# Row-sum reciprocals of an attention and feed-forward kernel: one VectorE reciprocal in place of a logarithm and an exponential on ScalarE

## The chip, the cores and the metric

The kernel runs on one core of a Trainium2 chip. The metric is the device time of one execution in microseconds. A core has a matrix engine (TensorE, PE in the profile, with its weight loads as PEld), VectorE (DVE), ScalarE (ACT), GpSimd (POOL) and a queue engine (SP). Each takes its own instructions strictly in order; they wait for one another by semaphores.

## The reference

The inputs are q, k, v of shape 8 x 8 x 576 x 64 (batch, head, row, depth), 16 further "beacon" keys and values for each head, and two weight matrices. The result is causal attention over beacons and rows, followed by a feed-forward layer with ELU:

```
scores = q @ concat(beacon_k, k).T / 8, causally masked (beacons are always seen)
a      = exp(scores - max);  a /= a.sum(-1) + 1e-9
x      = (a @ concat(beacon_v, v))  arranged as 4608 tokens x 512
out    = elu(x @ w_in) @ w_out      # w_in 512 x 2048, w_out 2048 x 512
```

The step that the change touches is the division by a.sum(-1), the row sums.

## The kernel before

The work runs through batches b = 0 to 7 and tiles t = 0 to 9 of the 4608 tokens. Attention of batch b fills x for the tiles that hold its tokens; the feed-forward steps of the tiles are interleaved with the attention of later batches. Nothing is left to a scheduler: a long string (lines 783 to 917) names each step in order, and each engine executes its own instructions in that order. The names below are those of the string.

Attention of a batch: `S` computes scores on PE (line 320) into PSUM tiles `sc`, `x` takes their exponentials on ACT (335) into `et`, `m` applies the causal mask on DVE (340). From batch 3 on, `D` adds up pieces of `et` on DVE (393) so that the row sums take fewer matmuls. `L` (line 401) computes the row sums on PE, as matmuls with a matrix of ones (377, 419), into the PSUM tile `lt`; each column of sums stands repeated over 32 partitions, so that it can be multiplied elementwise with the unnormalized output. `W` (448) computes that output on PE into `ut` (or `ub`, `ua`). `n` (429) is the step in question: it makes the reciprocals of the row sums in the SBUF tile `rl`. `M` (478, lines 471, 481, 488) multiplies `ut` by `rl` on DVE and writes `xT`, the input of the feed-forward part.

There are two groups of four heads per batch, so 16 steps `n`: one of 512 columns (`n.0.A`), one of 640 (`n.0.B`) and 14 of 576, all over 128 partitions in fp32.

Feed-forward: `F` (511) multiplies x by w_in on PE into PSUM banks `hps`; `e` (521) and `u` (526) take exponential and positive part on ACT; `k` (536) joins them on DVE into `gt`. For some tiles `r` (543) and `g` (548) do the second half on DVE instead. `G` (557), or for later tiles `Z` (578, sums on DVE), `Q` (621, matmuls) and `J` (630, 635, 637, copies and sums of results), multiply by w_out; the result goes out through the SP queue. The last two tiles use `P` (691), `K` (701, 704), `E`, `U`, `V` (713, 720, 730) in place of F, e, u, k.

What ties the engines: `e` and `r` tiles have three buffers, `hps`, `ops` and the scores' tag "S" two each. `lt` and `ut` are tiles of tag "S" and are read by DVE in `M`; `rl` has two buffers.

Of the kernel before, what the change touches and what calls it, by code (L numbers as in the profile page):

```python
# [11 lines left out]
AFT = mybir.ActivationFunctionType  # L12
# [5 lines left out]
def kernel(  # L18
# [11 lines left out]
    nc = tc.nc  # L30
# [110 lines left out]
    def load_v(b, js):  # L141
        if b not in vt:
            vt[b] = stage.tile([P, NKC, H, D], FP16, tag="v16", name="v16")
            nc.gpsimd.dma_start(  # L144
                out=vt[b][0:NB, 0, :, :], in_=beacon_v[b].rearrange("h n d -> n h d"))
        for j in js:
            r0 = NB if j == 0 else 0
            n = kc[j] - r0
            nc.gpsimd.dma_start(  # L149
                out=vt[b][r0:r0 + n, j, :, :],  # L150
                in_=v[b, :, ilo[j]:ilo[j] + n, :].rearrange("h s d -> s h d"),
            )
# [16 lines left out]
    for b in range(B):  # L169
        (nc.sync if b % 2 == 0 else nc.scalar).dma_start(  # L170
            out=bk32[NB * b:NB * (b + 1), :, :],
            in_=beacon_k[b].rearrange("h n d -> n h d"))
# [28 lines left out]
    @step  # L201
    def warm(n, rows=P):

        for _ in range(n):
            nc.tensor.matmul(
                out=w0, lhsT=zero[0:rows, 0:P], rhs=zero[0:rows, :], start=True, stop=True, skip_group_check=True)
# [221 lines left out]
    @step  # L428
    def n(b, g):
        src = lt[b, g]  # L430
        w = src.free_size()
        rl = rls[b, g] = attn.tile([P, 640], FP32, tag="rl", name="rl")
        dst = rl[:, 0:w]
        nc.scalar.activation(
            out=dst.rearrange("p (g c) -> p g c", g=2) if len(src.shape) == 3 else dst,
            in_=src, func=AFT.Ln, bias=0.0, scale=1.0)
        nc.scalar.activation(out=dst, in_=dst, func=AFT.Exp, bias=0.0, scale=-1.0)  # L437

    xt = {}

# [492 lines left out]
```

## Time and profile before

| | |
|---|---|
| median of 2 runs | 337.89 us (337.21 to 338.57) |
| span of the profiled execution (first to last instruction) | 335.3 us |
| busy: PE, ACT, DVE, POOL | 324.6, 282.5, 280.0, 87.9 us |
| granted TensorE clock, mean | 0.995 |

The profile gives the profiled execution by its span alone; its own time outside that is not shown. The span is 2.6 us below the median. Busy time is the time in which an engine executes; PE's is partly modelled, since matmuls overlap each other. "Idle before" is the idle time of an engine just ahead of an instruction, with the instruction of another engine that ended it.

### The profile page before, as it was taken

What the parts mean: (1) busy time and instruction counts of PE and PEld (TensorE: products, weight loads), DVE (VectorE), ACT (ScalarE), POOL (GpSimd) and SP (SyncE); (2) the same over time, 40 slices, a digit from 0 to 9 for tenths busy, and PEclk for the clock granted to TensorE, in tenths of its full rate; (3) what the DMA queues carried; (4) which work ended last, traced back from release to release, by engine and by line L of the source; (5) the groups of instructions that cost most, each with busy time, mean ns of one, the idle gap of its engine ahead of it and who ended that gap; (6) DMA issues with size and microseconds to landing.
All of it is one profiled execution on the core that took longest, in us unless ns stands there. A gap on an engine that the chain in (4) does not pass through costs nothing.

```text
span 335.3 us, 8722 instructions
## 1 busy us (share of the span) xinstructions
PE 324.6 (97%) x3561; PEld 206.8 (62%) x3561; DVE 280.0 (84%) x592; ACT 282.5 (84%) x460; POOL 87.9 (26%) x121
## 2 busy tenths in 40 slices
PE   7979899999999999999999999999999999999995
PEld 3546666454446555657555656556555888688784
DVE  3652988666899999997999889988999998998962
ACT  2998798899999999989898889897987677988930
POOL 8875749360049106500160060000000000000000
PEclk9997999999999999999999999999999999999999
DMA  9999999999939997996099495000101021010212
GB/s 114 146 174 178 165 186 186 157 147 176 149 52 170 175 139 61 171 149 105 33 140 139 104 100 139 3 33 31 39 27 34 31 65 65 31 65 31 65 63 96
DMA packets 129080, 34.65 MB, mean 103 GB/s; under 512 B 112912, under 2 KB 127504, under 8 KB 129040
## 3 DMA queue, kind: packets, MB, share of 16 engines
q0 software_dynamic: 94912, 18.49, 68.6%
q1 hardware_dynamic: 33408, 15.34, 21.2%
q8 instruction: 28, 0.46, 0.6%
q10 hardware_dynamic: 720, 0.26, 0.3%
q14 instruction: 12, 0.10, 0.1%
HBM read 37.22 MB, written 15.34 MB: 157 GB/s over the span
## 4 chain that ended last, share of the span: by engine, by line
PE 53%; DVE 20%; ACT 11%; DMA 7%; POOL 4%; issue 3%; ACTq 0%; POOLq 0%
PE ops L621 20%; PE hps L511 16%; DVE gt L536 6%; PE hps L691 6%; DVE qk L393 5%; ACT et L335 4%; ACT e L521 3%; PE sc L320 3%; PE ops L557 3%; ACT r L526 3%; PE ut L377 3%; DMA v<-in_v_dram 2%; DMA kst<-in_k_dram 2%; DMA w_out<-in_moe_w_out_dram 2%; DVE et L340 2%
## 5 line engine op out<-in xcount | busy, mean ns | idle before, releaser
L511 PE MATMUL hps<-xT,w_in 128*128 128x512 f16 (+1 forms) x544 | 120.2, 357 | 0.7 <-DMA w_in<-in_moe_w_in_dram 0.5
L335 ACT ACTIVATE et<-sc 128x1024 f16<-128x1024 f32 (+2 forms) x114 | 104.7, 978 | 5.3 <-PE sc L320 5.3
L621 PEld LDWEIGHTS <-gt 128*128 128x128 f16 x768 | 74.1, 98 | 18.7 <-issue 1.7
L521 ACT ACTIVATE e<-hps 128x512 f32<-128x512 f32 x120 | 72.5, 622 | 7.7 <-PE hps L511 5.9
L511 PEld LDWEIGHTS <-w_in 128*128 128x128 f16 x544 | 49.8, 98 | 45.3 <-issue 7.9
L536 DVE SCALAR_TENSOR_TENSOR gt<-e,r 128x512 f16<-128x512 f32 x108 | 71.9, 682 | 6.7 <-ACT r L526 4.4
L526 ACT ACTIVATE r<-hps 128x512 f16<-128x512 f32 x108 | 65.3, 623 | 7.7 <-PE hps L511 4.4
L621 PE MATMUL ops<-wt,gt 128*128 128x256 f16 x384 | 50.1, 273 | 0.0
L621 PE MATMUL ops<-w_out,gt 128*128 128x256 f16 x384 | 49.6, 273 | 0.4 <-DVE osb L635 0.3
L149 POOL DMA_DIRECT2D v<-in_v_dram x40 | 36.0, 1048 | 5.5 <-DMA w_out<-in_moe_w_out_dram 2.4
L340 DVE TENSOR_TENSOR et<-et,triu 128x512 f16<-128x512 f16 (+4 forms) x108 | 31.6, 331 | 1.5 <-ACT et L335 1.5
L578 DVE TENSOR_TENSOR gt<-gt 128x1024 f16<-128x1024 f16 x48 | 32.4, 684 | 0.3
L393 DVE TENSOR_TENSOR qk<-qk,et 128x672 f16<-128x672 f16 (+2 forms) x60 | 21.8, 368 | 0.9
L377 PEld LDWEIGHTS <-v 128*32 128x32 f16 (+1 forms) x800 | 17.0, 96 | 8.7 <-issue 0.8
L377 PE MATMUL ut<-et,v 128*32 128x464 f16 (+3 forms) x560 | 21.0, 296 | 0.0
L637 DVE TENSOR_TENSOR osb<-ops,sm 128x512 f32<-128x512 f32 x24 | 16.4, 682 | 4.3 <-issue 3.3
L471 DVE TENSOR_TENSOR xT<-ut,rl 128x672 f16<-128x672 f32 (+12 forms) x26 | 16.4, 668 | 1.7 <-ACT rl L437 1.1
L621 PE MATMUL ops<-w_out,s 128*128 128x256 f16 x128 | 17.1, 273 | 0.0
L730 DVE SCALAR_TENSOR_TENSOR gt<-e,r 128x512 f16<-128x512 f32 x24 | 16.0, 685 | 0.8 <-ACT r L720 0.7
L144 POOL DMA_DIRECT2D v<-in_beacon_v_dram x8 | 6.5, 812 | 38.4 <-PE ut L377 38.4
L557 PE MATMUL ops<-w_out,gt 128*128 128x512 f16 x64 | 16.0, 380 | 0.6 <-DMA w_out<-in_moe_w_out_dram 0.6
L621 PEld LDWEIGHTS <-s 128*128 128x128 f16 x128 | 12.4, 98 | 3.0
(108 smaller groups left out, 394.8 us busy)
## 6 DMA issues: line engine op xcount, KB each, us to landing
out_dram<-osb SPq DMA_DIRECT2D x35, 256.0 KB, 2.3
v<-in_v_dram POOLq DMA_DIRECT2D x24, 128.0 KB, 7.1
scr<-in_q_dram POOLq DMA_DIRECT2D x5, 576.0 KB, 13.8
scr<-in_k_dram POOLq DMA_DIRECT2D x5, 576.0 KB, 15.4
w_in<-in_moe_w_in_dram POOLq DMA_DIRECT2D x16, 128.0 KB, 7.5
w_out<-in_moe_w_out_dram POOLq DMA_DIRECT2D x4, 512.0 KB, 9.4
v<-in_v_dram POOLq DMA_DIRECT2D x8, 112.0 KB, 9.7
v<-in_v_dram POOLq DMA_DIRECT2D x8, 80.0 KB, 6.7
```

What stands on the lines that cost most here:

```text
L149: nc.gpsimd.dma_start(out=vt[b][r0:r0 + n, j, :, :], in_=v[b, :, ilo[j]:ilo[j] + n, :].rearrange("h s d -> s h d"),)
L335: nc.scalar.activation(out=ets[b, d][:, :, a - EC2 * d:e - EC2 * d], in_=sc[b, g][:, :, a - c0:e - c0], func=AFT.Exp, bias=0.0, scale=SCALE)
L340: nc.vector.tensor_tensor(out=o, in0=o, in1=i, op=ALU.mult)
L377: nc.tensor.matmul(out=t[32 * i:32 * (i + 1), a - qa:e - qa], lhsT=ones[0:kc[j], :] if half is None else v16[0:kc[j], j, h, 32 * half:32 * ...
L393: (nc.vector if eng == "v" else nc.gpsimd).tensor_tensor(out=o, in0=t[0:rows, :, a:e] if n == 0 else o, in1=t[0:rows, :, col:col + e - a], ...
L511: nc.tensor.matmul(out=h[:, n_, :], lhsT=w_in16[:, cc, P * fc:P * (fc + 1)], rhs=xt[k][:, cc, a - TT * k:e - TT * k], start=(cc == 0), sto ...
L521: nc.scalar.activation(out=eb[t, i], in_=flat(hp[t, i]), func=AFT.Exp, bias=0.0, scale=1.0)
L526: nc.scalar.activation(out=rb[t, i], in_=flat(hp[t, i]), func=AFT.Relu, bias=0.0, scale=1.0)
L536: nc.vector.scalar_tensor_tensor(out=half(t, i), in0=eb[t, i], scalar=1.0, in1=rb[t, i], op0=ALU.subtract, op1=ALU.min)
L557: nc.tensor.matmul(out=ob[t, tb_], lhsT=gt[:, fc, P * tb_:P * (tb_ + 1)], rhs=w_out16[:, fc, :], start=(fc == 0), stop=(fc == NFC - 1))
L578: (nc.vector if eng == "v" else nc.gpsimd).tensor_tensor(out=o_, in0=a_, in1=b_, op=op_)
L621: nc.tensor.matmul(out=xy[t, n_][:, qd, :], lhsT=lw[:, P * qd:P * (qd + 1)], rhs=wt_[:, c, :], start=(first and qd == 0 and c == 0), stop= ...
```

## The change

Step `n` loses its two ScalarE activations, the logarithm out of PSUM into `rl` (line 434) and the exponential of its negative in place (line 437), and gets one VectorE reciprocal out of PSUM into `rl`. The string of steps stays as it is, so the 16 reciprocals stand in VectorE's order where the word `n` stands: behind the VectorE instructions of the steps named earlier and ahead of those named later. All other instructions and their order on each engine are the same.

```diff
         dst = rl[:, 0:w]
-        nc.scalar.activation(
-            out=dst.rearrange("p (g c) -> p g c", g=2) if len(src.shape) == 3 else dst,
-            in_=src, func=AFT.Ln, bias=0.0, scale=1.0)
-        nc.scalar.activation(out=dst, in_=dst, func=AFT.Exp, bias=0.0, scale=-1.0)
+        nc.vector.reciprocal(
+            out=dst.rearrange("p (g c) -> p g c", g=2) if len(src.shape) == 3 else dst, in_=src)
```

## The prediction

> **What bounds the kernel now.** I read the busy line first, then the shares of the chain that ended last.
>
> ```profile
> PE 324.6 (97%) x3561; PEld 206.8 (62%) x3561; DVE 280.0 (84%) x592; ACT 282.5 (84%) x460; POOL 87.9 (26%) x121
> ...
> PE 53%; DVE 20%; ACT 11%; DMA 7%; POOL 4%; issue 3%; ACTq 0%; POOLq 0%
> ```
>
> PE leads, but no engine alone is the bound: the chain passes through PE, DVE and ACT in turn. VectorE's 84% is a mean over the whole span, so I asked for busy times by stretch, cut at 81.91, where the third batch begins its normalization, and at 318.24, where the last run of output matmuls begins. The columns are length, then PE, PEld, DVE, ACT and POOL busy.
>
> ```profile
> 19.03:81.91 62.88, 59.07 (x905) 35.59 (x908) 42.48 (x96) 55.91 (x82) 37.17 (x45) 0.97 1.72 172
> 81.91:318.24 236.33, 235.37 (x2317) 151.53 (x2306) 220.83 (x453) 210.24 (x357) 36.17 (x48) 1.00 0.72 85
> ```
>
> The reader is to see two regimes. Up to 82 us VectorE is idle for 20.4 us of 62.9. From 82 to 318 us it is idle for only 15.5 us of 236.3: it is 93% busy there. The normalization steps lie from 19 to 260 us, four pairs of activations in the first stretch and twelve in the second. After 318 us only the last matmuls and output copies remain.
>
> Next, what those pairs cost and who waits for them: groups with shapes kept apart, and VectorE's waits in the second stretch.
>
> ```profile
> L434 ACT ACTIVATE rl<-lt 128x576 f32<-128x576 f32 x14 | 9.7, 693 | 1.3 <-PE lt L377 1.3
> L437 ACT ACTIVATE rl<-rl 128x576 f32<-128x576 f32 x14 | 9.6, 683 | 0.4
> ```
>
> ```profile
> DVE xT L471 <- ACT rl L437: 5.0, 6, 1.7
> DVE gt L536 <- ACT r L526: 2.4, 4, 1.1
> DVE gt L536 <- ACT e L521: 1.6, 1, 1.6
> DVE et L340 <- ACT et L335: 1.5, 2, 1.3
> ```
>
> Of VectorE's 15.5 us idle, 5.0 us (six times) end with the exponential of this step. Waits for other ACT results make up another 6.9 us (these three rows and smaller ones of 0.7, 0.5 and 0.2 us). The rest, 3.6 us, is PE and issue.
>
> **What is removed.** ScalarE loses 14 pairs of 693 + 683 ns, one of 660 + 630 ns and one of 700 + 740 ns: 22.1 us, of which 12 x 1.38 = 16.5 us in the second stretch. There ACT is 89% busy, and the chain gives it only 11% of the span, so I count no gain for it beyond the shorter waits of VectorE above. The hand-over from ACT to DVE was 0.04 us at the one pair I looked at (exponential's end 57.63, multiplication's start 57.67): nothing.
>
> **What is added.** 16 reciprocals on VectorE, 14 of 576 columns, one of 512, one of 640. No row shows a VectorE reciprocal, so its price has to be bounded. The nearest rows are the multiplications by `rl`, which also read fp32 out of PSUM:
>
> ```profile
> L471 DVE TENSOR_TENSOR xT<-ut,rl 128x928 f16<-128x928 f32 x2 | 2.2, 1116 | 0.0
> ...
> L471 DVE TENSOR_TENSOR xT<-ut,rl 128x256 f16<-128x256 f32 x2 | 0.8, 414 | 0.0
> ```
>
> (1116 - 414) / (928 - 256) = 1.045 ns per element, and 414 - 256 x 1.045 = 146 ns fixed. One pass over 576 elements is thus 0.75 us, the lower end. But a multiplication is one step of arithmetic and a quotient is not. [...] With one pass of 1.045 ns per element for each step, six steps are 0.146 + 6 x 576 x 1.045 ns = 3.76 us, and eight are 4.96 us, my upper end. [...] I take six: I find it hard to see a full-precision quotient made at a multiplication's rate, and between six and eight the cheaper way is the nearer to the only rate that a row shows. The 512 and 640 columns are then 3.36 and 4.16 us, all 16 together 60.2 us.
>
> [...]
>
> **Second stretch.** 12 x 3.76 = 45.1 us come on an engine with 15.5 us to spare. Its work becomes 220.8 + 45.1 = 265.9 us, so the stretch can't be shorter than that: at least 29.6 us longer even with no idle time left. What goes and what stays of the idle time is a choice. The 5.0 us for this step's exponential go, since it is made on VectorE itself; some of the 6.9 us for other ACT results goes, as ACT is lighter and VectorE later. The 3.6 us of PE and issue stay. New waits come: behind each reciprocal stand masks (340), joins `k` (536), sums (578, 393) and the multiplications of `M`; F waits for M, e and u for F, and the next k for them, a round trip in which VectorE may run dry. Between 3.6 and 15.5 us left idle I take 9, that is 97% busy: the stretch grows by 45.1 - 6.5 = 38.6 us. No reciprocal lies between 263 and 318 us, but VectorE is 95% busy there too (56.2 of 59.1 us from 259 on), so the lateness goes through to the last joins, sums and matmuls.
>
> **First stretch.** Four reciprocals, 15.0 us, on an engine that is idle for 20.4 us but at other moments. What counts is how much later the multiplications start. The row sums of the second batch's second pair are there at 60.89, and `M` began at 62.29; with the reciprocal it starts at 64.65, 2.4 us later, and PE's weight load for F already waited 0.32 us for that `M`. The pair at 56.26 gives about 2.5 us likewise. The two of the first batch (19.03 and 31.98) lie among transfers that the chain waits for, 8.3 us for v from 12.2, 8.0 us for k from 23.6 and 7.8 us for w_out from 32.4, which cover most of their 2 to 3 us; that cover ends at 40.3. Ends: 0 and 10 us (four times 2.5). I take 5, the two uncovered ones.
>
> **Sum.** 38.6 + 5.0 = 43.6 us on the profiled execution's span of 335.3, so 378.9 us; with the 2.6 us by which the median stands over that span, 381.5 us, rounded to **381 us**.
>
> **Rivals.**
>
> *One pass (not slower).* The reciprocal runs at the multiplication's rate, 0.75 us. For it speaks that it is a single instruction; against it the arithmetic above. Then VectorE gets 12 x 0.75 = 9.0 us in the second stretch, loses the 5.0 us and, say, half of the 6.9 us: +0.5 us. In the first, the two uncovered pairs end 1.36 - 0.75 = 0.6 us sooner each: -1.2 us. About 337 us; with all of the 6.9 us gone and some gain from a lighter ACT, below 331. It decides by the reciprocal's duration: at 8.5 / 12 = 0.7 us the second stretch breaks even, and at (8.5 + 6.8) / 12 = 1.3 us it is 2% slower (2% of 337.9 is 6.8 us, about what a measurement of this kernel can tell from no change).
>
> [...]
>
> *The queue.* Six steps, but the reciprocals also hold up ready work: VectorE takes its instructions in order, and a reciprocal that waits for its row sums blocks the masks and joins behind it, where before only `M` waited. Priced by the mean of the nine waits for this step in the whole trace (12.1 us), 1.34 us, 16 times: +21 us, about 403 us. Against it: a VectorE that is itself late finds the row sums ready.
>
> *Hidden behind PE.* PE at 97% could seem to cover VectorE. It can't, beyond the 15.5 us: 265.9 us of work do not fit into 236.3. I give this no chance at six steps; at one step it is the first rival.
>
> **How the numbers follow.** Forecast 0.56, eight steps 0.22, the queue 0.07, one pass 0.15 (0.11 within 2%, 0.04 faster). Slower by over 2% is thus 0.85, within 0.11, faster 0.04. The forecast's own range: no idle left and no early cost, 337.9 + 29.6 = 367.5; all idle kept and 10 us early, 393. The range for 8 in 10 leaves out one pass and the far end of the queue: at the low end five steps, 3.16 us, with no idle left (12 x 3.16 - 15.5 = 22.4 us, 360), rounded to 362; at the high end the eight steps with a few us more of kept idle time, 406.
>
> **What would show it.** The reciprocal's group of 14 has a mean near 3.76 us (0.75 and 4.96 for the rivals). VectorE's busy time goes from 280 to about 340 us and ACT's to 260. In the stretch from the third batch's normalization to the last matmuls VectorE is some 97% busy and about 275 us long. The chain's DVE share goes from 20% to over half, and PE and its weight loads wait for DVE by tens of us in total, where all such waits for `xT` come to 2.0 us now (1.4, 0.3 and 0.3). If the group's mean is as forecast and the time is not, the step that failed is the idle time left on VectorE. A mean under 1.3 us makes the whole forecast wrong.

## The result and the profile after

The changed kernel takes 410.25 us, median of 2 runs (409.74 to 410.75), against 337.89: a ratio of 1.217, 95% interval 1.212 to 1.222. It is slower by 72.4 us; 43.6 had been forecast, and 410 lies 4 us above the range. The ratios of the experiments leave out two executions that ran 2 to 3% longer than the others of their kernel, one of e7 and one of the kernel before.

The busy line and the shares of the chain of the changed kernel (line numbers are two lower than before from line 438 on):

```profile
PE 351.8 (86%) x3561; PEld 215.9 (53%) x3561; DVE 341.8 (84%) x608; ACT 266.7 (65%) x428; POOL 88.6 (22%) x121
...
PE 45%; DVE 41%; ACT 6%; issue 4%; POOL 1%; DMA 1%; DVEq 0%; ACTq 0%; POOLq 0%
```

VectorE's share of the chain went from 20% to 41%; over half had been forecast. Its busy time went from 280.0 to 341.8 us and ACT's from 282.5 to 266.7; about 340 and 260 had been forecast. The reader should stop at PE: the same 3561 matmuls are busy for 351.8 us in place of 324.6. Nothing was added to PE, so its matmuls became slower.

VectorE's group of reciprocals, shapes kept apart:

```profile
L434 DVE RECIPROCAL rl<-lt 128x576 f32<-128x576 f32 x14 | 52.5, 3751 | 6.3 <-PE lt L377 6.2
```

The price is 3.75 us; the forecast had 3.76. Busy times by stretch, cut at the same places as before (the third batch's first step `n`, and the last run of output matmuls; columns are length, then PE, PEld, DVE, ACT and POOL busy, granted clock, DMA share, GB/s):

```profile
19.00:97.14 78.14, 64.74 (x888) 38.23 (x886) 59.18 (x98) 50.98 (x73) 36.37 (x45) 0.87 1.51 149
97.14:390.50 293.36, 256.52 (x2341) 158.17 (x2330) 265.85 (x468) 199.51 (x335) 37.21 (x48) 0.92 0.53 65
```

The first stretch grew by 15.3 us (from 62.88), the second by 57.0 (from 236.33). VectorE's work in the second is 265.85 us, and 265.9 had been forecast. But it is idle there for 27.5 us, more than the 15.5 before, where 9 had been forecast. The second stretch is thus 91% VectorE work, not the 97% of the forecast. The column before the last two is the granted TensorE clock: 0.87 and 0.92, where it was 0.97 and 1.00.

PE's longest waits in total, first the longest of the kernel before, then three of the changed kernel:

```profile
PE sc L320 <- ACT et L335: 1.8, 3, 0.7
```

```profile
PE sc L320 <- DVE xT L469: 22.3, 12, 3.5
PE hps L509 <- DVE gt L546: 6.3, 2, 3.2
PE ops L619 <- DVE sm L628: 5.8, 2, 4.2
```

PE stops twelve times at a step of scores, for 22.3 us, until VectorE has made the multiplications behind the reciprocal. The scores need a PSUM buffer of tag "S", and both are held by `lt` and `ut`.

One such stop closely, PE's timeline and then single microseconds around it (PE, PEld, DVE, ACT, POOL busy, granted clock):

```profile
74.61 1.04 PE L555 MATMUL ops<-w_out,gt 128*128 128x512 f16 x4
77.64 0.61 PE L320 MATMUL sc<-qk 64*128 64x64 bf16 x4 [2.00 <-DVE xT L469]
78.41 1.89 PE L509 MATMUL hps<-xT,w_in 128*128 128x512 f16 x4 [0.16 <-DVE xT L469]
...
81.13 1.04 PE L555 MATMUL ops<-w_out,gt 128*128 128x512 f16 x4
```

```profile
76.00:77.00 1.00, 0.00 (x0) 0.00 (x0) 1.00 (x1) 0.00 (x0) 1.00 (x2) 1.00 2.47 158
77.00:78.00 1.00, 0.36 (x4) 0.13 (x4) 0.96 (x3) 0.00 (x0) 1.00 (x2) 0.80 2.47 158
78.00:79.00 1.00, 0.84 (x4) 0.28 (x3) 1.00 (x3) 0.71 (x1) 1.00 (x1) 0.50 2.45 156
79.00:80.00 1.00, 1.00 (x4) 0.15 (x1) 1.00 (x3) 0.32 (x1) 0.46 (x1) 0.50 2.41 153
80.00:81.00 1.00, 1.00 (x9) 0.44 (x8) 1.00 (x3) 0.67 (x2) 0.00 (x0) 0.50 2.13 136
81.00:82.00 1.00, 1.00 (x8) 0.41 (x5) 0.16 (x1) 1.00 (x2) 0.00 (x0) 1.00 2.27 145
```

PE stops for 2.00 us, and when it goes on the granted clock is 0.50 for about 3.4 us. Four matmuls of 512 columns take 1.89 us there, and 1.04 us at full clock on either side. So this stop is paid twice: while it lasts, and in the matmuls after it. By the mean granted clock (0.920 of 407.6 us; cut into pieces of 0.1 us, it is 1.00 or 0.50 in all but those at a change) some 65 us ran at half clock; before it was 3.4 us (0.995 of 335.3).

### The profile page after: what moved, and what is told of

Read it like the earlier page. It is cut to its first block, busy times and chain, and to the rows that moved or that the text cites. A ratio compares the mean times of both kernels' runs of the same rounds, so it can differ in the third digit from the quotient of the medians.

```text
span 407.6 us, 8702 instructions
## 1 busy us (share of the span) xinstructions
PE 351.8 (86%) x3561; PEld 215.9 (53%) x3561; DVE 341.8 (84%) x608; ACT 266.7 (65%) x428; POOL 88.6 (22%) x121
## 4 chain that ended last, share of the span: by engine, by line
PE 45%; DVE 41%; ACT 6%; issue 4%; POOL 1%; DMA 1%; DVEq 0%; ACTq 0%; POOLq 0%
PE hps L509 15%; PE ops L619 14%; DVE rl L434 14%; DVE gt L534 8%; DVE qk L393 5%; PE hps L689 5%; PE sc L320 5%; DVE et L340 3%; DVE xT L469 3%; ACT et L335 3%; DVE gt L576 2%; ACT e L519 2%; PE ops L555 2%; ACT r L524 2%; DVE r L541 1%
## 5 line engine op out<-in xcount | busy, mean ns | idle before, releaser
L509 PE MATMUL hps<-xT,w_in 128*128 128x512 f16 (+1 forms) x544 | 132.5, 385 | 8.9 <-DVE gt L546 6.3
L519 ACT ACTIVATE e<-hps 128x512 f32<-128x512 f32 x120 | 72.3, 621 | 31.1 <-PE hps L509 24.3
L619 PEld LDWEIGHTS <-gt 128*128 128x128 f16 x768 | 75.8, 100 | 29.0 <-issue 8.5
L509 PEld LDWEIGHTS <-w_in 128*128 128x128 f16 x544 | 52.9, 104 | 60.6 <-issue 26.1
L534 DVE SCALAR_TENSOR_TENSOR gt<-e,r 128x512 f16<-128x512 f32 x108 | 72.0, 682 | 10.3 <-ACT r L524 6.6
L434 DVE RECIPROCAL rl<-lt 128x576 f32<-128x576 f32 (+1 forms) x15 | 56.7, 3778 | 8.4 <-PE lt L377 8.3
L619 PE MATMUL ops<-w_out,gt 128*128 128x256 f16 x384 | 52.1, 281 | 3.3 <-DVE osb L635 3.3
L619 PE MATMUL ops<-wt,gt 128*128 128x256 f16 x384 | 51.4, 277 | 4.1 <-DVE gt L576 2.5
L619 PE MATMUL ops<-w_out,s 128*128 128x256 f16 x128 | 18.8, 291 | 4.2 <-DVE sm L628 4.2
L320 PE MATMUL sc<-kst 64*128 64x208 bf16 (+13 forms) x160 | 13.2, 271 | 9.7 <-DVE xT L469 9.3
L320 PE MATMUL sc<-qst 64*128 64x336 bf16 (+13 forms) x160 | 12.9, 270 | 9.0 <-DVE xT L469 9.0
## 6 DMA issues: line engine op xcount, KB each, us to landing
scr<-in_q_dram POOLq DMA_DIRECT2D x5, 576.0 KB, 13.4
```

The lines of the kernel that those rows point to most:

```text
L320: nc.tensor.matmul(out=s[:, h, a - c0:e - c0], lhsT=t[D * h:D * (h + 1), 1, P * j:P * (j + 1)], rhs=t[D * h:D * (h + 1), 0, NB + qa + a - ...
L434: nc.vector.reciprocal(out=dst.rearrange("p (g c) -> p g c", g=2) if len(src.shape) == 3 else dst, in_=src)
L509: nc.tensor.matmul(out=h[:, n_, :], lhsT=w_in16[:, cc, P * fc:P * (fc + 1)], rhs=xt[k][:, cc, a - TT * k:e - TT * k], start=(cc == 0), sto ...
L519: nc.scalar.activation(out=eb[t, i], in_=flat(hp[t, i]), func=AFT.Exp, bias=0.0, scale=1.0)
L534: nc.vector.scalar_tensor_tensor(out=half(t, i), in0=eb[t, i], scalar=1.0, in1=rb[t, i], op0=ALU.subtract, op1=ALU.min)
L619: nc.tensor.matmul(out=xy[t, n_][:, qd, :], lhsT=lw[:, P * qd:P * (qd + 1)], rhs=wt_[:, c, :], start=(first and qd == 0 and c == 0), stop= ...
```

## The experiments

Each was timed against the kernel before on the same chip, which took 336.8 to 337.6 us there. The first theory (called hold below) was that the harm comes from the two PSUM buffers that the reciprocal holds; its rival (load), that 60 us more on VectorE cost that wherever they stand; a third (clock), that the half clock makes up the surplus over the forecast.

**e1: the place without the price.**

```diff
-        nc.vector.reciprocal(out=dst, in_=src)
+        nc.vector.tensor_scalar(out=dst, in0=src, scalar1=0.0, scalar2=1.0 / 300.0, op0=ALU.mult, op1=ALU.add)
```

> Step n writes a constant (0 x sum + 1/300) with one VectorE instruction in the reciprocal's place, so the normalization by the row sums is left out; place, order and tiles are those of the changed kernel, only the duration differs (about 0.75 us at 576 columns in place of 3.75). Hold theory (the reciprocal stands between the row sums and the multiplications that give back two PSUM buffers, PE stops for it and its clock falls): 333 to 342 us, half-clock time back below 10 us. Load theory (VectorE's extra occupancy costs what it takes, wherever it stands): also 333 to 345 us. If moving the step to VectorE had a price of its own apart from the duration, it would be above 350 us.

342.0 us, ratio 1.014 (1.012 to 1.017), clock 1.0. The instruction:

```profile
L434 DVE TENSOR_SCALAR rl<-lt x15: 744/751/825, 30.4 to 262.2; 128x576 f32<-128x576 f32 x14, 128x640 f32<-128x640 f32 x1
```

One pass is 0.75 us, the forecast's lower end. With the duration gone, 1.4% is left of a loss of 21.7%: nearly all of it is the reciprocal's duration, and a price of the move apart from that (above 350 us) is excluded. The hold and the load theory had both foreseen this. And even a reciprocal at one pass would not have gained: 22 us less on ACT brought nothing.

**e2: the load without the hold.** The kernel before, with both activations, plus:

```diff
+        done[b, g] = done.get((b, g), 0) + 1      # at the end of step M
+        if done[b, g] == 2:
+            nc.vector.reciprocal(out=rls[b, g][:, 0:w], in_=rls[b, g][:, 0:w])
```

> The kernel before, with its two ScalarE activations, plus one VectorE reciprocal of the same size in place on rl behind both multiplications of each group (16 in all, about 3.75 us each; its result is not used). The load on VectorE is that of the changed kernel, but nothing that frees PSUM waits for it directly. Hold theory: 367 to 385 us (capacity alone, as the forecast had it), mean clock above 0.96, PE's waits for xT below 5 us. Load theory: 400 us or more. Clock theory (the surplus over the forecast is only PE at half clock after any pause): about 385 to 395 us with a clock of 0.93 to 0.95.

401.2 us, ratio 1.190 (1.186 to 1.195), clock 0.957. The busy line:

```profile
PE 342.6 (86%) x3559; PEld 212.7 (53%) x3561; DVE 343.6 (86%) x608; ACT 285.0 (71%) x460; POOL 88.5 (22%) x121
```

PE's waits for `xT` are down to 1.0 us, as the hold theory had said, but the time is not: its 367 to 385 is wrong. The load theory's 400 or more holds, narrowly. The clock theory's 385 to 395 is missed as well.

**e3: the hold taken away.** For the 14 groups of 576 columns:

```diff
+            nc.scalar.copy(out=dst, in_=src)                       # step n
+            copy_out(b, g, 0, QA, <first 112 columns of output>)    # PSUM to xT, ScalarE
+            nc.vector.reciprocal(out=dst, in_=dst)
+            copy_out(b, g, QA, S, t[:, :, 0:S - QA])                # end of step W
-                in0=u[:, :, o - qa:o - qa + w],                     # step M
+                in0=y,                                              # y: the slice of xT itself
```

> The changed kernel, but for the 14 groups of 576 columns ScalarE copies the row sums from PSUM to rl and the unnormalized output from PSUM to xT (fp16) as soon as PE has made them; the reciprocal and the multiplications then work in place in SBUF, so both PSUM buffers come free without VectorE. ScalarE gets some 28 us more. Hold theory: PE's 22 us of waits for xT at the scores go, mean clock above 0.96, 365 to 385 us. Load theory: 400 us or more, since VectorE's work is the same. Clock theory alone gives no number of its own here.

418.4 us, ratio 1.241 (1.237 to 1.245). PE's and VectorE's waits:

```profile
PE hps L525 <- DVE xT L486: 10.3, 3, 5.2
PE ops L635 <- DVE osb L651: 9.7, 3, 6.1
PE hps L525 <- ACT e L535: 9.3, 8, 1.9
PE hps L525 <- DVE gt L562: 9.1, 3, 5.9
```

```profile
DVE rl L440 <- ACT rl L438: 22.4, 10, 3.3
```

The stops at the scores did go (this list has none of them), but PE then stopped at the next things that VectorE owed it: `xT`, `gt`, `osb`. And VectorE now waited 22.4 us for the copies of the sums. The PSUM buffers were only the first place at which PE met the delay. This run alone is no clean test, since the copies brought VectorE a wait of their own; together with e2 it rules out hold as the main cause of the loss.

**e4, e9, e10: matmuls in the stops.** Step W's matmuls, which overwrite `ut` with the same values, are made again: three times in all where W stands (e4), or once (e9) or twice (e10) more just ahead of PE's next request for a buffer.

```diff
-            for half in range(2):
+            for half in (0, 1) * 3:
                 quad(b, g, QA, S, t[:, half, 0:S - QA], half, True)
```

> The changed kernel with the 40 matmuls of step W (1.3 us) made three times over, with the same result, for 14 groups: some 37 us more matmul work for PE, most of it in the time in which it waits for the reciprocal. Clock theory (pauses of some 3 us halve the granted clock, 66 us at half in the changed kernel, which costs up to 33 us): half-clock time falls below 30 us and the time to 385 to 402 us in spite of the added work. Hold theory without a part for the clock: 410 to 425 us.

> The changed kernel with the 40 matmuls of step W repeated once more (1.3 us, same result, 14 times, 18 us of added PE work) exactly where PE would next stop for a PSUM buffer, behind both the row sums and the output of the group. VectorE's work is that of the changed kernel. If the half clock (65 us of it in the changed kernel, 55 us of which are PE work on the chain, so at most 27 us lost) is what took the time past the forecast: half-clock time below 30 us and 388 to 400 us. If the half clock only fills time in which PE would have waited anyway: 408 us or more.

> The same with two repeats at each stop (2.6 us, 37 us of added PE work). Clock theory: half-clock time still lower, below 20 us, time 385 to 402 us, since the second repeat runs past the end of many stops. If the half clock costs nothing: 412 us or more.

e4: 405.1 us, ratio 1.204 (1.199 to 1.209), clock 0.977. e9: 407.2 us, ratio 1.210 (1.203 to 1.218), clock 0.961. e10: 416.3 us, ratio 1.238 (1.232 to 1.243), clock 0.971. The clock rose in all three, but none came into the clock theory's range, and e10's time is the one expected if the half clock cost nothing (412 us or more). Against that, e4 is 5 us faster than the changed kernel in spite of 37 us more of matmuls. Much of the added work stood where PE did not stop, so gain and cost were mixed: not decided. e12 was made for that.

**e5, e6: blocks and pieces.** The kernel before plus 64 reciprocals of 144 columns on a private tile, four in a row behind each group (e5) or one at a time between other VectorE steps (e6).

```diff
+        if todo:                       # e6: ahead of each step k, g, D, Z, J, m; e5: four times behind M
+            todo.pop()
+            nc.vector.reciprocal(out=junk, in_=junk)
```

> The kernel before plus, behind each group's multiplications, four VectorE reciprocals of 144 columns in a row on a tile that nothing else touches (64 in all, about 1.05 us each, 67 us; result unused). Nothing waits for their result, so they are load in blocks of 4.2 us. Additive theory (each block stops PE and ScalarE for most of its length, because only two or three buffers let them run ahead, and the lost time is not made up): 398 to 410 us. Capacity theory of the forecast: 372 to 390 us.

> The same 64 reciprocals on the private tile, but one at a time, each between two other VectorE steps, so that no block is longer than about 1.1 us; VectorE's load is that of the kernel with the blocks. If the length of the block is what does the harm (buffers that cover about 1 us but not 4, and a clock that falls after long pauses): 365 to 388 us, clock above 0.98. If the added load counts in full wherever it stands: 398 to 410 us.

e5: 410.5 us, ratio 1.215 (1.207 to 1.222), at the upper end of the additive theory's range. e6: 391.0 us, ratio 1.156 (1.153 to 1.160), between the two numbers. Pieces of 1.04 us are better than blocks of 4.2 us by 5.8% of the time before, some 20 us, but most of the cost stays: the buffers do not cover the load even in pieces. VectorE is also busy for less time in e6, 341.1 us against 348.1 with the same instructions; these 7 us were not separated from the length of the blocks.

**e7, e11: the price in steps.** The reciprocal on half and on three quarters of the columns, the constant in one pass on the rest.

```diff
+            nc.vector.reciprocal(out=dst[:, 0:w // 2], in_=src[:, 0:w // 2])          # e11: 3 * w // 4
+            nc.vector.tensor_scalar(out=dst[:, w // 2:w], in0=src[:, w // 2:w],
+                scalar1=0.0, scalar2=1.0 / 300.0, op0=ALU.mult, op1=ALU.add)
```

> The changed kernel with the reciprocal on half of the columns and the constant 1/300 in one pass on the other half (the normalization of those is left out): about 1.95 + 0.45 = 2.4 us a step. Between the one-pass kernel (342 us at 0.75 us) and the changed kernel (410 us at 3.75 us), a constant slope of 68 us for 16 x 3.0 us gives 380 us. If short pauses are covered and the clock falls only after long ones: 362 to 373 us, half-clock time below 20 us.

> The changed kernel with the reciprocal on three quarters of the columns and the constant in one pass on the rest (their normalization is left out): about 2.85 + 0.30 = 3.15 us a step. Load alone, one to one from the half kernel (363 us at 2.4 us): 363 + 16 x 0.75 = 375 us. Straight line from there to the changed kernel (410 us at 3.75 us): 389 us with some 40 us at half clock. The clock theory asks that the time above 375 us be about half of the half-clock time beyond the 9 us of the half kernel.

e7: 363.2 us, ratio 1.075 (1.071 to 1.079), clock 0.991; e11: 388.2 us, ratio 1.152 (1.146 to 1.158), clock 0.956. Up to 2.4 us a step the cost is less than the load: 21 us for 16 x 1.65 = 26 us over e1. From there to 3.15 us it is 25 us for 12, and to 3.75 us another 22 for 10. The curve bends where the clock starts to fall. With half-clock time as twice the shortfall of the mean clock times the span, e7 has 6.5 us, e11 34 us: half of the difference is 14 us, and e11 lies 13 us above the 375 us of load one to one, as the clock theory asked.

**e8: the first stretch alone.**

```diff
+        if b < 2:
             nc.vector.reciprocal(...)
+        else:
+            <the two activations>
```

> The VectorE reciprocal only in batches 0 and 1 (four of the 16), the two ScalarE activations in the others. By the forecast's term for the first stretch: +5 us (0 to 10), about 342 us. By the trace of the changed kernel, where that stretch grew by 15 us, as much as the four reciprocals take: 350 to 354 us, half-clock time about 20 us.

351.9 us, ratio 1.044 (1.040 to 1.048), clock 0.979: 14.5 us for four reciprocals of 15 us. The forecast's term of 5 us is wrong, also by its upper end of 10; the 350 to 354 us read from the trace holds. In its profile PE is idle for 9.1 us more than before (349.5 - 329.7 against 10.7) and its matmuls take 5.1 us more, so the stops alone would have stayed within the term's range.

**e12: matmuls only in stops that the trace shows.** As e9, but where the changed kernel's trace has PE stop at the scores for 1.9 us or more:

```diff
+    FILL = {(1, 1): 1, (1, 0): 1, (2, 1): 1, (3, 1): 2, (4, 1): 2, (5, 0): 2, (5, 1): 1, (6, 0): 1}
+    def Y(b, g):
+        for _ in range(FILL.get((b, g), 0)):
+            for half in range(2):
+                quad(b, g, QA, S, ut[b, g][:, half, 0:S - QA], half, True)
```

> The changed kernel with step W's 40 matmuls repeated only where its trace shows PE stopping at the scores for 1.9 us or more, once (stops near 2 us) or twice (2.8 to 3.5 us): 11 repeats of 1.3 us, 14.5 us, in 8 stops of 20.3 us together, so that to first order no matmul is added to PE's time outside a stop. Nothing else differs. If the half clock costs time: half-clock time some 30 to 40 us in place of 66, the other matmuls' busy time 10 to 14 us lower, and the time 393 to 402 us. If it only fills time in which PE would wait: 408 to 412 us.

396.8 us, ratio 1.178 (1.173 to 1.182). The clock of the profiled execution is 0.974, so 20 us at half clock; the other five have 0.961 to 0.965, some 28 to 31 us. The intervals of this ratio and the changed kernel's, 1.212 to 1.222, are far apart: some 14.5 us of useless matmuls (eleven repeats of about 1.3 us) made it 13 us faster. Its busy line and PE's wait at the scores, and the granted clock in 40 slices, the changed kernel's first and this one's below:

```profile
PE 349.1 (89%) x3999; PEld 220.7 (56%) x4001; DVE 341.8 (87%) x608; ACT 265.5 (67%) x428; POOL 88.2 (22%) x121
```

```profile
PE sc L320 <- DVE xT L477: 8.2, 11, 1.1
```

```profile
PEclk9967889899689999688989698999999979999999
```

```profile
PEclk9978899999899999999999999999999889999999
```

VectorE's work is the changed kernel's to the tenth, 341.8 us. PE's is lower by 2.7 us although 14.5 us were added: its other matmuls take 17.2 us less. Most of the sixes, sevens and eights have become nines. What remains is in slices 3 to 5, 11, 32 and 33; the stops in other places (up to 4.2 us, at `ops`) were not filled.

## Why the prediction was wrong, point by point

The direction, the engine and the price of the reciprocal were right: 3.75 us measured for 3.76, VectorE's work in the second stretch right to 0.1 us. But no row and no run shows a number of steps, neither the six of the price nor the five and eight of the range, so a hit to 0.01 us is partly luck; what the runs show in their place is the cost per element (6.27 ns, six times the 1.045 of a multiplication), not how the quotient is made. The rivals fall with the price: the group's mean of 3.75 us excludes one pass at 0.75 us and the upper end of 4.96, and waits of reciprocals for their row sums are 9.5 us in the changed kernel (8.3 for `lt`, 1.2 for `la`), not 21.

The step that failed is the turning of that load into time, "Between 3.6 and 15.5 us left idle I take 9", together with "I take 5" for the first stretch. Measured, VectorE is left idle for 27.5 us and the first stretch grew by 15.3 us; the 18.5 and 10.3 us between make up the whole miss of 28.8. The prediction had named this step itself as the one to fail if the price held. Both terms took it that PE's matmuls go on costing what they cost. The span can be split into PE's busy and idle time:

| kernel | span, us | PE busy | PE idle | mean clock |
|---|---|---|---|---|
| before | 335.3 | 324.6 | 10.7 | 0.995 |
| changed | 407.6 | 351.8 | 55.8 | 0.920 |
| e7, half the columns | 361.1 | 329.7 | 31.4 | 0.991 |
| e11, three quarters | 388.5 | 341.5 | 47.0 | 0.956 |
| e12, filled stops | 394.1 | 349.1, of which 14.5 added | 45.0 | 0.974 |

Of the 72.3 us of span, 45.1 are new stops of PE and 27.2 are slower matmuls. The stops alone nearly equal the 43.6 us of the forecast, but that is partly luck: the forecast had VectorE's idle time in the second stretch fall by 6.5 us, and it rose by 12.0. By stretch they are 9.6 us in the first (13.4 against 3.8; forecast 5) and 35.9 in the second (36.8 against 1.0; forecast 38.6). The missing term is the clock, 5.7 us in the first stretch and 21.2 in the second. (The stretches hold 17 fewer and 24 more matmuls than before, so these figures by stretch are good to 1 or 2 us.) That it costs time, and does not merely fill waits, is shown by e12: 17.2 us of it taken away, at the price of 14.5 us of added work in stops, made the kernel 13 us faster. At that rate all 27.2 us would be worth some 21 us, a time near 389; that is an estimate from e12, no run shows it. The rate is not fixed either: the other five executions of e12 have 7 to 10 us more at half clock than the profiled one, and their spans are only 0.3 to 2.3 us longer, so part of the half clock falls where PE would have waited anyway.

The second thing that the forecast missed is why the load is not absorbed. VectorE's idle time was taken as room that a late VectorE would use up. It did not: in e2, where no PSUM buffer waits for the reciprocal, VectorE's idle time is 55.4 us (399.0 - 343.6), as before (55.3). PE at 97% had been set aside with the words that it can't cover VectorE. It can't, but it also can't make up for a stop: with 10.7 us idle it has nothing to catch up with, and each stop delays what VectorE waits for next. This is read from the split above; no run with less matmul work tried it.

The hold on the PSUM buffers, formed as a theory after the result, explains where PE stops but not how much is lost (e2, e3). What stays open is how e12's remaining 60 us divide between VectorE's load and the length of its blocks; e5 and e6 put the blocks at up to some 20 us.

The reciprocals of 144, 288, 432 and 576 columns took 1.04, 1.95, 2.85 and 3.75 us (e6, e7, e11 and the changed kernel), which is 6.27 ns per element and 0.14 us fixed.

## What to carry to other kernels

An engine that is 97% busy had little room here to make up for stops: 45.1 of the 72.3 us lost are new stops of PE, and e2 lost its time although VectorE stood idle for 55.4 us. Before work is moved to an engine that feeds the matrix engine, price the longest single instruction against the buffers in between, and add the granted clock: after three of five stops near 2.0 us at the scores here, and after all eight of 2.85 us and more, matmuls ran at a clock of 0.50 (1.89 us in place of 1.04 for four of 512 columns), so that such a stop was paid a second time. A reciprocal cost five times one pass here (3.75 against 0.75 us); the two activations, 1.38 us on ScalarE, were the cheaper way.

## What the runs showed of the hardware

The half clock came after stops shorter than the time for which it lasts. In the changed kernel stops at the scores of 2.00, 2.00, 2.03, 2.85, 3.04 and 3.47 us were followed by it (ending at 77.64, 114.70, 250.49, 162.61, 209.92 and 228.87); stops of 2.02 us (71.05) and 1.92 us (273.48) were not. So three of the five stops near 2.0 us there were followed by it, and so were all eight of 2.85 us and more (the three at the scores, and 3.19, 3.16, 3.11, 3.34 and 4.17 us at other steps, ending at 37.44, 54.14, 102.42, 181.07 and 331.72).

The length of a stop alone does not tell them apart. The changed kernel has twelve stretches at half clock. They begin at 22.98, 36.63, 53.70, 77.59, 101.48 us and so on up to 330.18, whole multiples of 3.41 us apart, and each lasts 3.41 or 6.83 us; the only one of the kernel before lasts 3.41 us (25.37 to 28.78). In pieces of that length, counted from 22.98 us in both directions, PE stands idle for 1.63 to 2.85 us of 3.41 in the twelve at full clock that half clock follows, and for at most 1.93 us in those that full clock follows, so the two ranges overlap. Seven of the pieces (the column before the last two is the granted clock):

```profile
67.36:70.77 3.41, 1.66 (x43) 0.89 (x40) 3.41 (x3) 1.08 (x2) 0.68 (x1) 1.00 2.03 158
70.77:74.18 3.41, 3.13 (x74) 2.11 (x78) 2.10 (x4) 2.06 (x3) 0.00 (x0) 1.00 1.81 116
74.18:77.59 3.41, 1.46 (x24) 0.52 (x12) 3.38 (x3) 0.00 (x0) 2.59 (x4) 1.00 2.34 156
77.59:81.00 3.41, 3.20 (x16) 1.01 (x16) 3.41 (x7) 1.69 (x3) 1.87 (x1) 0.50 2.35 150
81.00:84.42 3.42, 3.42 (x29) 1.57 (x26) 0.16 (x1) 3.16 (x5) 0.00 (x0) 1.00 2.38 156
139.04:142.45 3.41, 1.49 (x8) 0.48 (x5) 3.41 (x2) 0.91 (x2) 0.00 (x0) 1.00 2.46 156
142.45:145.86 3.41, 2.38 (x24) 1.62 (x25) 3.41 (x8) 1.85 (x4) 0.00 (x0) 1.00 2.12 194
```

The stop that ends at 77.64 puts 1.95 us into the third piece, and half clock follows; the one that ends at 71.05, as long, puts 1.75 us into the first and 0.28 into the second. Even a stop of 2.51 us was not followed by half clock (at `ops`, ending at 143.04): it puts 1.92 us into the sixth piece and 0.59 into the seventh, which holds another stop of 0.44 us. None of the twelve pieces ahead of half clock was idle throughout, and of two stops of the same length one was paid once and the other twice. This is read from one execution; no run moved a stop to try it.

VectorE's reciprocal took the same time from PSUM (3.75 us) as from SBUF (3.75 us in e3), and its cost per element is constant from 144 to 640 columns (1.04 to 4.16 us).
